# A two-layer transformer-like stack on one core: six phi(q) buffers, two norms moved to VectorE, the first load split, one output unit moved

## The chip, the cores and the metric

The kernel runs on one core of one Trainium2 chip. The metric is the device time in microseconds (us) of one execution, the median of several runs. The engines are named as the profile names them: PE is TensorE (matmuls), PEld its weight loads, DVE is VectorE, ACT is ScalarE, POOL is GpSimd, SP is SyncE, which here only issues DMAs. "SPq" and "ACTq" are the issuing queues.

## The reference

Four layers over x of 2048 rows and 1024 columns: linear attention A, gated bilinear unit B, and both once more with the same weights. Each is added to x after a layer norm.

```python
def _A_ref(x, wqkv, wo):                       # 32 heads of 32
    q, k, v = split_heads(x @ wqkv)
    phi = lambda t: jnp.where(t > 0, t + 1, jnp.exp(t)) + 1e-6
    pq, pk = phi(q), phi(k)
    kv = jnp.einsum("bhsd,bhse->bhde", pk, v)
    z = jnp.einsum("bhsd->bhd", pk)
    num = jnp.einsum("bhqd,bhde->bhqe", pq, kv)
    den = jnp.einsum("bhqd,bhd->bhq", pq, z)[..., None] + 1e-6
    return merge_heads(num / den) @ wo
def _B_ref(x, w_gate, w_up, w_down):           # 1024 -> 3584 -> 1024
    g, u = x @ w_gate, x @ w_up
    return (g * u) @ w_down
x = x + _A_ref(_layernorm(x), A_wqkv, A_wo)
x = x + _B_ref(_layernorm(x), B_w_gate, B_w_up, B_w_down)
x = x + _A_ref(_layernorm(x), A_wqkv, A_wo)
x = x + _B_ref(_layernorm(x), B_w_gate, B_w_up, B_w_down)
```

Head splitting and merging are written as names here.

## The kernel before

All buffers are placed by hand in a few large tiles (K0 to K7, W, MX, TX, ST, XT0, XT1), PSUM is used as eight banks Q0 to Q7, and the order of the instructions on each engine is the order in which the Python code emits them. x stays in SBUF as X, 16 row tiles of 128 x 1024, in four groups of four tiles. Each tile's normalised rows are transposed by a DMA (tx, L301, issued on SP), for the first few tiles on PE.

**A layer of A** (layer_A, layers 0 and 2) runs: the k units (32, a tile and a half of the columns each); then xk units, phi(k) transposed times the normalised x; then 32 q units, q[2t] and q[2t+1] for the two halves of tile t. A q unit is eight matmuls into one bank (proj_mm, L340), then phi: ACT takes the exponential (L328, or L323 and L324 in the "split" form), DVE finishes it (L329 and L330, or L325 and L326) into the tile's buffer from pqb. Each q unit then calls flush, which runs one half of the previous tile's division: den_sums (L420 to L423) after q[2t], den_divide (L428) and the transpose of the buffer after q[2t+1]. The buffers of pqb are taken in turn; so a tile's first phi write waits until the transpose of the tile that had the buffer before has read it.

With the q units of the last five tiles the kernel mixes the "kv copies" (kvo_unit: one matmul L447 into Q5 to Q7 in turn, and a scaled copy by ACT, L448) and the first output units. An output unit o[i] is eight matmuls (L459) and add_x on DVE (L451), which adds the bank into X. There are 32; the first six are ordered so that three with n = 0 come first. PE's banks come from mm_tile, a running count taken modulo rotation[0]: five while the kv copies use Q5 to Q7, eight otherwise.

Other work is hung on the output units. jobs[i] runs after o[i]: in layer 0, o[2] to o[8] each bring one scan (scan_step, L217: ACT squares a 512 KB chunk of weights and sums it; 42 chunks, the last ones w_down, each fetched by a DMA issued on ACT, L209, into a buffer that an earlier scan leaves), o[3] to o[6] the conversion of the first gate and up weights (L489) and their sums (L492), o[10] and o[15] the scale of w_down from the scans (scale_sum, L226 and L227; scale_pow, whose matmul is L232, then POOL's power L234). The list norm holds the layer norms of groups 0 and 1 for the next layer, one step after each of o[8] to o[17], the rest spread over o[18] to o[27]. For each tile a norm on ACT (ln_act) is three passes over the tile (L285 mean, L289 variance, L295 apply), between them small POOL steps (L286, L290 to L292), and then the transpose. The form used elsewhere, ln_stats and ln_apply, has DVE take statistics (L251, L255), POOL two steps (L257, L259), and DVE apply (L269).

**A layer of B** (layer_B, layers 1 and 3) computes its three matrix products by a scheme with seven half-size products instead of eight. At its start the products 1 and 2 (L527) use group 0's transposed x; the products 6 and 5 use sums of the two groups, t_fill (L492, into TX). After products 1, 6 and 7 ACT copies the banks (L545, L549) into SN, which lies in MX and W. MX is otherwise used in layer A for zb, its first quarter; its other three quarters are free there.

Of the kernel before, what the change touches and what calls it, by code (L numbers as in the profile page):

```python
# [37 lines left out]
def kernel(  # L38
# [11 lines left out]
    nc = tc.nc  # L50
    P = 128
    S, D = A_x.shape[1], A_x.shape[2]
# [8 lines left out]
    TPG = G // P  # L61
    NB = 512
# [12 lines left out]
    X = const.tile([P, NT, D], BF16, tag="X", name="X")  # L75
# [3 lines left out]
    MX = const.tile([P, 4 * D], BF16, tag="MX", name="MX")  # L79
    K = [const.tile([P, BLK], BF16, tag=f"K{i}", name=f"K{i}") for i in range(8)]  # L80
    W = const.tile([P, 8 * D], BF16, tag="W", name="W")
# [8 lines left out]
    def tail(i, j):  # L90
        return K[i][:, HEAD + j * D:HEAD + (j + 1) * D]
# [9 lines left out]
    pk = [tail(0, 2)] + [tail(i, j) for i in (1, 2, 3, 4, 5) for j in range(3)]  # L101
    sk = K[0][:, HEAD:HEAD + 2 * D].bitcast(F32)
    zb = MX[:, 0:D]
    pqb = [W[:, i * D:(i + 1) * D] for i in range(3)]
    pb = [W[:, 6 * D + i * NB:6 * D + (i + 1) * NB] for i in range(4)]
    eb = [W[:, 3 * D + i * NB:3 * D + (i + 1) * NB] for i in range(3)]
    kvt = W[:, 5 * D:6 * D].rearrange("p (c f) -> p c f", f=P)
# [4 lines left out]
    xn_c = {TPG + i: tail(i, 0) for i in range(4)}  # L112
    xn_b = [ST[:, t % TPG * D:(t % TPG + 1) * D] for t in range(NT)]
# [6 lines left out]
    count = {}  # L120
# [5 lines left out]
    x_view = A_x[0].rearrange("(t p) d -> p t d", p=P)  # L126
# [7 lines left out]
    def load(dst, src):  # L134
        nc.sync.dma_start(out=dst, in_=src)
# [9 lines left out]
    def load_x(t):  # L145
        load(X[:, t, :], x_view[:, t, :])

    load_x(0)
    load_x(1)
    for k in range(0, KD, 2):  # L150
        load(wk[0][:, k:k + 2, :], wqkv_v[:, k:k + 2, D:D + NB])
# [96 lines left out]
    def bn(t, c):  # L248
        if c == 0:
            stat[t] = [small.tile([P, 2, 6], F32, tag="st", name="st")]  # L250
        nc.vector.bn_stats(out=stat[t][0][:, c, :], in_=X[:, t, c * NB:(c + 1) * NB])  # L251

    def moments(t):
        mv = small.tile([P, 2], F32, tag="mv", bufs=2 * TPG, name="mv")
        nc.vector.bn_aggr(out=mv[:], in_=stat[t][0][:])  # L255
        ve = small.tile([P, 1], F32, tag="ve", name="ve")
        nc.gpsimd.tensor_scalar(out=ve[:], in0=mv[:, 1:2], scalar1=1e-5, scalar2=None, op0=ALU.add)  # L257
        rstd = small.tile([P, 1], F32, tag="rstd", bufs=2 * TPG, name="rstd")
        nc.gpsimd.tensor_tensor(out=rstd[:], in0=ve[:], in1=mhalf[:, 0:1], op=ALU.pow)  # L259
        stat[t] = (mv, rstd)  # L260

    def ln_stats(t):
        bn(t, 0)
        bn(t, 1)
        moments(t)

    def ln_apply(t, xn):
        mv, rstd = stat.pop(t)
        nc.vector.tensor_scalar(out=xn, in0=X[:, t, :], scalar1=mv[:, 0:1], scalar2=rstd[:],  # L269
                                op0=ALU.subtract, op1=ALU.mult)  # L270
# [9 lines left out]
    def ln_act(t, xn):  # L280

        sm, nm, ss, ve, rstd, off = (small.tile([P, 1], F32, tag=n_, name=n_) for n_ in ("sm", "nm", "ss", "va", "rs", "of"))

        def mean():
            nc.scalar.activation(out=xn, in_=X[:, t, :], func=ACT.Identity, accum_out=sm[:])  # L285
            nc.gpsimd.tensor_scalar(out=nm[:], in0=sm[:], scalar1=-1.0 / D, scalar2=None, op0=ALU.mult)  # L286

        def var():
            nc.scalar.activation(out=xn, in_=X[:, t, :], func=ACT.Square, bias=nm[:], accum_out=ss[:])  # L289
            nc.gpsimd.tensor_scalar(out=ve[:], in0=ss[:], scalar1=1.0 / D, scalar2=1e-5, op0=ALU.mult, op1=ALU.add)  # L290
            nc.gpsimd.tensor_tensor(out=rstd[:], in0=ve[:], in1=mhalf[:, 0:1], op=ALU.pow)
            nc.gpsimd.tensor_tensor(out=off[:], in0=nm[:], in1=rstd[:], op=ALU.mult)  # L292

        def apply():
            nc.scalar.activation(out=xn, in_=X[:, t, :], func=ACT.Identity, scale=rstd[:], bias=off[:])  # L295
        return mean, var, apply

    def tx(xn, t, slot):

        tl = t % TPG  # L300
        nc.sync.dma_start_transpose(out=xT[slot][:, :, tl * P:(tl + 1) * P], in_=xn)  # L301
# [106 lines left out]
    def flush():  # L408
        if later:
            later.pop(0)()  # L410
# [43 lines left out]
    def out_unit(t, n):  # L454
        def run():
            ps = mm_tile()
            tl = t % TPG
            for c in range(KD):
                nc.tensor.matmul(out=ps, lhsT=xT[t // TPG][:, c, tl * P:(tl + 1) * P].bitcast(F16), rhs=KVo[n][:, c, :],  # L459
                                 start=(c == 0), stop=(c == KD - 1))  # L460
            add_x(t, n, ps)
        return run
# [41 lines left out]
    def prep(n, eng=nc.vector):  # L504
        return [lambda: convert(n, 0), lambda: convert(n, 1), lambda: sums(n, 0, eng), lambda: sums(n, 1, eng)]
# [96 lines left out]
    def do(units):  # L602
        for u in units:
            u()
# [12 lines left out]
        tr = [lambda t=t: tx(dst[t], t, slot_) for t in ts]  # L617
        return st + [ap[0], ap[1], tr[0], ap[2], tr[1], ap[3], tr[2], tr[3]]

    def norm_act(g, slot_, dst):  # L620

        f = [ln_act(t, dst[t]) for t in range(g * TPG, (g + 1) * TPG)]
        tr = [lambda t=t: tx(dst[t], t, slot_) for t in range(g * TPG, (g + 1) * TPG)]
        out_ = []
        for i in range(TPG + 2):
            for j, k in ((i, 0), (i - 1, 1), (i - 2, 2)):
                if 0 <= j < TPG:
                    out_.append(f[j][k])
                    if k == 2:
                        out_.append(tr[j])  # L630
        return out_
# [3 lines left out]
    def layer_A(li):  # L635
# [103 lines left out]
        kvo = [lambda c=c: kvo_unit(c % KD, c // KD) for c in range(2 * KD)]  # L739
        o = [out_unit(t, n) for t in range(NT) for n in range(2)]  # L740
        o = [o[i] for i in (0, 2, 4, 1, 3, 5)] + o[6:]
        norm = norm_act(0, 0, xn_b) + norm_act(1, 1, xn_c)
        jobs = {3: prep(0)[0:1], 4: prep(0)[1:2], 5: prep(0)[2:3], 6: prep(0)[3:4]}
        if first_A:
            for i, f in ((10, lambda: scale_sum(2, 3)), (9, dp[0][0]), (15, lambda: scale_pow(2, 3)), (13, dp[1][0])):
# [4 lines left out]
        def out_next(n=1):  # L750
            for _ in range(n):
                i = count["o"] = count.get("o", -1) + 1
                o[i]()
                do(jobs.get(i, []))
                if 8 <= i < 18:
                    do(norm[i - 8:i - 7])
# [3 lines left out]
        for i in range(6):  # L760
            q[22 + i]()
            do(kvo[8 * i // 3:8 * (i + 1) // 3])
            if i > 2:
                out_next()
        rotation[0] = 8
        for i in range(4):
# [2 lines left out]
        flush()  # L769
        out_next()  # L770
        flush()
        out_next(6)
        down = list(dp[0][1:]) + list(dp[1][1:]) if first_A else []
        late = norm[10:]
        for i in range(10):
# [16 lines left out]
    def layer_B(li):  # L792
        last = li == 3
        R = [Q[2 * i:2 * i + 2] for i in range(4)]
        for ps in range(2):
# [165 lines left out]
            R = [R[2], R[1], R[3], R[0]]  # L961

    layer_A(0)
    layer_B(1)
    layer_A(2)
    layer_B(3)

# [29 lines left out]
```

## Time and profile before

| | us |
|---|---|
| median of 3 runs | 1499.27 (1498.31 to 1500.75) |
| the profiled execution, its own time | 1501.54 |
| its span, first to last instruction | 1499.8 |
| PE busy | 1485.4 |
| DVE busy | 1053.0 |
| ACT busy | 747.2 |

Where the stages of the profiled execution lie: layer 0 to 248.3 us, layer 1 to 759.6, layer 2 to 989.0, layer 3 to the end. The granted clock of PE is 0.999 in the mean. The page gives each engine's busy time and its share of the span; since PE's is 99%, what can be read from the waits is where the remaining time lies, and from the windows where the clock was not full.

### The profile page before, as it was taken

How to read it: one execution, taken by the hardware profiler on the slowest of the kernel's cores; microseconds unless marked ns; L12 is line 12 of the kernel's file. 1: busy time of each engine (PE TensorE's matmuls, PEld its weight loads, DVE VectorE, ACT ScalarE, POOL GpSimd, SP SyncE). 2: the span in 40 equal slices, each digit the busy share in tenths (PEclk: the TensorE clock that was granted, in tenths of full speed). 3: DMA queues.
4: the chain of work that ended last, by engine and by line, in shares of the span. 5: the costliest groups of instructions: out<-in, count | busy, mean ns of one | idle time of the engine just before them, and what ended most of it. 6: DMA issues, size and time to landing. Idle time of an engine off the chain costs nothing.

```text
span 1499.8 us, 18432 instructions
## 1 busy us (share of the span) xinstructions
PE 1485.4 (99%) x6997; PEld 676.1 (45%) x6997; DVE 1053.0 (70%) x1813; ACT 747.2 (50%) x934; POOL 67.3 (4%) x187
## 2 busy tenths in 40 slices
PE   9999999999999999999999999999999999999999
PEld 3444444444444444444444444444444444444444
DVE  7768767888866577767388567667776846777533
ACT  4988587777601366650022446846664015666300
POOL 3100002000000000001010000200000100000000
PEclk9999999999999999999999999999999999999999
DMA  7966947667647333336660115433333763333442
GB/s 216 248 190 179 233 93 197 200 200 212 195 163 216 84 85 85 85 127 175 183 168 1 20 33 124 69 94 85 91 95 110 211 190 97 85 84 85 147 167 86
DMA packets 276905, 202.80 MB, mean 135 GB/s; under 512 B 101968, under 2 KB 264016, under 8 KB 273232
## 3 DMA queue, kind: packets, MB, share of 16 engines
q1 hardware_dynamic: 261456, 182.74, 43.8%
q10 hardware_dynamic: 15360, 18.88, 4.2%
q8 instruction: 55, 0.90, 0.3%
q14 instruction: 34, 0.28, 0.1%
HBM read 160.43 MB, written 17.04 MB: 118 GB/s over the span
## 4 chain that ended last, share of the span: by engine, by line
PE 82%; ACT 2%; DVE 1%; issue 1%; DMA 1%; POOL 0%; SPq 0%; ACTq 0%; DVEq 0%
PE Q L527 45%; PE Q L828 23%; PE Q L340 7%; PE Q L459 4%; PE Q L355 4%; ACT K L217 0%; DMA K<-in_B_w_down_dram 0%; DVE X L451 0%; ACT K L289 0%; PE Q L439 0%; ACT K L285 0%; DMA XT<-K 0%; ACT K L448 0%; ACT W L324 0%; DVE den L421 0%
## 5 line engine op out<-in xcount | busy, mean ns | idle before, releaser
L527 PEld LDWEIGHTS <-K 128*128 128x128 f16 x3136 | 306.7, 98 | 373.6 <-issue 2.4
L527 PE MATMUL Q<-XT,K 128*128 128x512 bf16 (+1 forms) x1792 | 405.7, 379 | 0.0
L828 PE MATMUL Q<-K,K 128*128 128x512 f16 (+2 forms) x1582 | 340.4, 377 | 0.0
L527 PE MATMUL Q<-TX,K 128*128 128x512 f16 x1344 | 308.4, 379 | 2.8 <-ACT W L549 1.4
L489 ACT ACTIVATE K<-K,fac 128x2048 f16<-128x2048 bf16 x112 | 218.4, 2000 | 128.1 <-DMA K<-in_B_w_gate_dram 127.2
L828 PEld LDWEIGHTS <-K 128*128 128x128 f16 x1582 | 154.3, 98 | 184.5
L492 DVE TENSOR_TENSOR K<-K 128x1024 f16<-128x1024 f16 (+1 forms) x244 | 157.3, 666 | 34.2 <-ACT K L489 32.3
L492 DVE TENSOR_TENSOR W<-MX,Q 128x512 f16<-128x512 f32 x176 | 116.4, 684 | 30.0 <-ACT MX L549 18.6
L328 ACT ACTIVATE W<-Q 128x512 bf16<-128x512 f32 x90 | 52.8, 595 | 137.7 <-PE Q L340 127.9
L340 PE MATMUL Q<-K,K 128*128 128x512 bf16 x512 | 115.6, 380 | 3.6 <-DVE X L451 3.6
L549 ACT COPY MX<-Q 128x512 f32<-128x512 f32 x120 | 69.2, 584 | 96.0 <-PE Q L527 96.0
L340 PE MATMUL Q<-K,XT 128*128 128x512 bf16 x512 | 114.6, 379 | 1.4 <-DMA XT<-ST 0.7
L492 DVE TENSOR_TENSOR W<-W,Q 128x512 f16<-128x512 f32 x160 | 105.4, 684 | 13.3 <-ACT W L549 7.1
L549 ACT COPY W<-Q 128x512 f32<-128x512 f32 x104 | 60.3, 584 | 73.5 <-PE Q L527 73.4
L492 DVE TENSOR_TENSOR K<-K,K 128x512 f16<-128x512 f16 (+1 forms) x148 | 87.7, 597 | 4.2
L492 DVE TENSOR_TENSOR K<-W,Q 128x512 f16<-128x512 f16 x56 | 38.4, 686 | 71.9 <-PE Q L527 71.9
L340 PEld LDWEIGHTS <-K 128*128 128x128 bf16 x512 | 49.9, 98 | 64.1 <-issue 4.7
L835 DVE SCALAR_TENSOR_TENSOR W<-Q,kap,X 128x512 f32<-128x512 f32 x32 | 24.0, 750 | 77.6 <-PE Q L828 77.6
L340 PEld LDWEIGHTS <-XT 128*128 128x128 bf16 x512 | 49.5, 98 | 61.1 <-ACT XT L316 1.4
L531 DVE TENSOR_TENSOR K<-W 128x512 f16<-128x512 f16 x168 | 71.4, 425 | 5.8
L217 ACT ACTIVATE K<-K 128x2048 bf16<-128x2048 bf16 x37 | 70.6, 1908 | 3.4 <-DMA K<-in_B_w_down_dram 2.4
L545 ACT COPY MX<-Q 128x512 f32<-128x512 f32 x56 | 32.3, 588 | 63.4 <-PE Q L527 63.4
(111 smaller groups left out, 1226.3 us busy)
## 6 DMA issues: line engine op xcount, KB each, us to landing
K<-WD SPq DMA_DIRECT2D x28, 1792.0 KB, 7.4
K<-in_B_w_gate_dram SPq DMA_DIRECT2D x70, 512.0 KB, 4.2
K<-in_B_w_up_dram SPq DMA_DIRECT2D x56, 512.0 KB, 5.1
K<-in_A_wqkv_dram SPq DMA_DIRECT2D x10, 1024.0 KB, 7.8
K<-in_B_w_up_dram ACTq DMA_DIRECT2D x12, 512.0 KB, 4.0
K<-in_B_w_down_dram ACTq DMA_DIRECT2D x11, 512.0 KB, 4.6
K<-in_B_w_down_dram SPq DMA_DIRECT2D x10, 512.0 KB, 5.4
WD<-K SPq DMA_DIRECT2D x10, 512.0 KB, 3.0
```

What stands on the lines that cost most here:

```text
L217: nc.scalar.activation(out=scan_buf[i], in_=scan_buf[i], func=ACT.Square, accum_out=acc[:, m, c:c + 1])
L328: nc.scalar.activation(out=e, in_=ps, func=ACT.Exp)
L340: nc.tensor.matmul(out=ps, lhsT=xt[:, k, tl * P:(tl + 1) * P], rhs=w[:, k, :], start=(k == 0), stop=(k == KD - 1))
L355: nc.tensor.matmul(out=ps, lhsT=xn_a[t][:, j * P:(j + 1) * P], rhs=pk[t][:, n * NB:(n + 1) * NB], start=(t == 0), stop=(t == NT - 1))
L459: nc.tensor.matmul(out=ps, lhsT=xT[t // TPG][:, c, tl * P:(tl + 1) * P].bitcast(F16), rhs=KVo[n][:, c, :], start=(c == 0), stop=(c == KD - 1))
L489: nc.scalar.activation(out=b.bitcast(F16), in_=b, func=ACT.Copy, scale=fac[:, m:m + 1])
L492: eng.tensor_tensor(out=o, in0=a, in1=b, op=op)
L527: nc.tensor.matmul(out=pair[m], lhsT=stationary(n, p, m, k), rhs=moving[p][:, k, :], start=(p in (1, 2, 5) and k == 0), stop=(k == KH - 1) ...
L531: nc.vector.tensor_tensor(out=hA[i][:, u, :], in0=gu[:, 0, :], in1=gu[:, 1, :], op=ALU.mult)
L545: nc.scalar.copy(out=snaps[u, 1][:, m, :], in_=a[m])
L549: nc.scalar.copy(out=snaps[u, p][:, m, :], in_=a[m])
L828: nc.tensor.matmul(out=ps_[:, lo:hi], lhsT=act[:, u, j * P:(j + 1) * P], rhs=w[:, u, lo:hi], start=(p in (1, 2, 5) and u == 0), stop=(u == ...
```

## The change

Four edits.

1. pqb has six buffers instead of three: the three in W, and the three free quarters of MX.
2. The first tile of x is loaded as two halves of 512 columns, one issued on SP as before, the other on ACT.
3. norm_act gets a number m: the first m tiles of the group take the norm on ACT, the others ln_stats and ln_apply on DVE, in the same steps of the list. Group 0 keeps all four tiles on ACT, group 1 only two.
4. While the kv copies run, an output unit follows q[25] and q[27] but no longer q[26]. All later pairs of output units thus begin one unit earlier in number, and after the second flush seven units follow instead of six, so that 18 have run before the loop over o[18 + i].

```diff
-    pqb = [W[:, i * D:(i + 1) * D] for i in range(3)]
+    pqb = [W[:, i * D:(i + 1) * D] for i in range(3)] + [MX[:, i * D:(i + 1) * D] for i in range(1, 4)]
...
-    load_x(0)
+    nc.sync.dma_start(out=X[:, 0, 0:NB], in_=x_view[:, 0, 0:NB])
+    nc.scalar.dma_start(out=X[:, 0, NB:D], in_=x_view[:, 0, NB:D])
...
-    def norm_act(g, slot_, dst):
-
-        f = [ln_act(t, dst[t]) for t in range(g * TPG, (g + 1) * TPG)]
-        tr = [lambda t=t: tx(dst[t], t, slot_) for t in range(g * TPG, (g + 1) * TPG)]
+    def norm_act(g, slot_, dst, m):
+
+        ts = range(g * TPG, (g + 1) * TPG)
+        f = [ln_act(t, dst[t]) for t in ts[:m]]
+        f += [(lambda t=t: ln_stats(t), lambda: None, lambda t=t: ln_apply(t, dst[t])) for t in ts[m:]]
+        tr = [lambda t=t: tx(dst[t], t, slot_) for t in ts]
...
-        norm = norm_act(0, 0, xn_b) + norm_act(1, 1, xn_c)
+        norm = norm_act(0, 0, xn_b, TPG) + norm_act(1, 1, xn_c, 2)
...
             do(kvo[8 * i // 3:8 * (i + 1) // 3])
-            if i > 2:
+            if i == 3 or i > 4:
                 out_next()
         rotation[0] = 8
...
         flush()
         out_next()
         flush()
-        out_next(6)
+        out_next(17 - count["o"])
```

## The prediction, made before the change was run

> **What bounds the kernel now.** I read the page first, then the waits by engine, then the timeline around every place where TensorE waits. The page:
>
> ```profile
> PE 1485.4 (99%) x6997; PEld 676.1 (45%) x6997; DVE 1053.0 (70%) x1813; ACT 747.2 (50%) x934; POOL 67.3 (4%) x187
> ```
>
> The span is 1499.8 us, so TensorE idles for only 14.4 us. Nothing that shortens DVE or ACT work as such can pay; only an idle gap of TensorE, or matmuls run at a lower clock, can be won. The waits, by engine and line (us in total, times, longest):
>
> ```profile
> DVE W L330 <- DMA K<-W: 4.1, 2, 2.8
> ...
> PE Q L340 <- DVE X L451: 3.6, 1, 3.6
> PE Q L527 <- ACT W L549: 1.4, 2, 1.2
> PE Q L527 <- DVE TX L492: 1.3, 1, 1.3
> ...
> PE Q L459 <- DVE W L330: 0.8, 1, 0.8
> ```
>
> Both waits on DVE work of 3.6 and 0.8 us lie in the first attention layer, where the kv copies and the last q units run together. Timeline of DVE and of TensorE there (start, length, instruction, idle before it and who ended it):
>
> ```profile
> 171.83 0.69 DVE L330 SCALAR_TENSOR_TENSOR W<-Q,W 128x512 bf16<-128x512 f32 x1 [1.30 <-DMA K<-W]
> 179.97 0.69 DVE L330 SCALAR_TENSOR_TENSOR W<-Q,W 128x512 bf16<-128x512 f32 x1 [2.79 <-DMA K<-W]
> ...
> 184.04 1.89 PE L459 MATMUL Q<-K,XT 128*128 128x512 bf16 x8 [0.80 <-DVE W L330]
> 189.50 2.44 PE L340 MATMUL Q<-K,K 128*128 128x512 bf16 x8 [3.57 <-DVE X L451]
> 191.73 4.79 PE L459 MATMUL Q<-K,XT 128*128 128x512 bf16 x16
> ```
>
> L330 writes phi(q) of tile 11 (and 12) into the buffer that tile 8 (and 9) left, and waits for that tile's transpose to be read out. In that stretch the transposes land late: "DMA to landing" of L301 between 150 and 260 us is
>
> ```profile
> DMA to landing us min/median/max: 3.0/4.3/10.0
> ```
>
> DVE is otherwise back to back from 165 to 191, so the 1.30 + 2.79 = 4.09 us push everything behind. Then the clock, by windows (window, us, busy time of each engine, granted clock, DMA share, GB/s):
>
> ```profile
> 184.00:188.00 4.00, 1.89 (x8) 0.78 (x8) 3.87 (x6) 1.54 (x3) 0.00 (x0) 1.00 0.34 66
> 188.00:192.00 4.00, 2.50 (x9) 1.04 (x9) 3.73 (x8) 1.80 (x1) 0.00 (x0) 0.84 0.00 0
> 192.00:196.00 4.00, 4.00 (x15) 1.61 (x14) 2.89 (x6) 3.55 (x7) 0.00 (x0) 0.74 0.34 66
> ```
>
> After the 3.57 us gap the granted clock is 0.84 and 0.74. The step into layer 1:
>
> ```profile
> 248.31 3.62 PE L527 MATMUL Q<-XT,K 128*128 128x512 bf16 x16
> 253.19 2.98 PE L527 MATMUL Q<-TX,K 128*128 128x512 f16 x13 [1.26 <-DVE TX L492]
> ...
> 250.18 1.22 DVE L492 TENSOR_TENSOR TX<-XT,XT 128x2048 f16<-128x2048 bf16 x1 [2.71 <-DMA XT<-K]
> ```
>
> The norms of the second group end late on ACT, their transposes land at 249.9, and the first sum waits. In layer 2 (ACT, the kv copies L448):
>
> ```profile
> 926.81 1.84 ACT L448 ACTIVATE K<-Q,rz 128x512 bf16<-128x512 f32 x3
> 929.85 0.60 ACT L323 ACTIVATE W<-Q 128x512 bf16<-128x512 f32 x1 [1.19 <-PE Q L340]
> ```
>
> Here ACT waits for TensorE, and TensorE has no gap beyond 0.2 us.
>
> **What the Trainium skill says.** "TensorE: Matmul & The Clock Gate", section "What's actually happening": after an idle window of about 3.4 us the clock falls to half. The trace agrees: lower clock after 3.57 us, none after 1.26 us. "Perfetto Trace Analysis", section "Tensor Engine Instruction": ACT, DVE and GpSimd are strict first-in-first-out; the 4.09 us that pass through L330 to everything behind it agree. "DMA: Bandwidth & Descriptors", section "Issuing engines are not separate DMA queues": issuing from another engine saves only issue time.
>
> **The change, part by part.** Pitches, start to next start, from the timelines: L329 0.33, L330 0.61, the den sums L420 to L423 2.46, L428 1.13, L325 0.38, L326 0.34, add_x 0.60 us; a q or out unit 1.727, a kv matmul 0.216, L323 0.49, L324 0.57, a kv copy 0.61 us.
>
> *Six buffers.* Tiles 11 and 12 now overwrite what tiles 5 and 6 left, long transposed. Both DMA waits go, and DVE is 4.09 us earlier from q unit 24 on: L330 of q25 at 183.30 − 4.09 = 179.2, add_x of the first out unit at 180.95, q26's L326 at 181.92, its den sums done at 184.7. The ACT inputs were ready before (L323 at 178.47). The 0.80 us wait goes.
>
> *The out unit moved from q26 to behind q28.* TensorE in layer 0: q26 176.54, three kv to 178.9, q27 at once to 180.64, three kv. Their banks (three in turn) come free with ACT's copies at 179.53 to 181.37, so the third kv waits 0.35. Out unit 2 ends at 183.4; q28 follows. By the bank counts (q22 is the 81st tile; five in rotation, then eight) q28 now takes bank 0 (q26's, read by 179.6) and no longer the bank of the second out unit, on which it waited 3.57. That bank falls to the unit after next, o3: ready 186.83, add_x done at 187.3, 0.45 us. Before, nine units and eight kv matmuls, 15.54 + 1.73 = 17.27 us, took 172.66 to 196.36 = 23.70; now they take 17.27 + 0.80. Gain 5.6 us, about 2.1 of it the clock.
>
> *What is late next.* ACT's chain of squares over w_down (scans 35 to 41) moves one out unit later in order: scan 35 behind q28's L326, 188.0 instead of 190.2. In pitches (scan 2.0, convert 2.0, DMA issue 0.4) ACT then runs: scans 35 and 36, issue, convert to 194.4; q29's pair to 195.5; scan 37, issue of fetch 39 at 197.5, convert, scan 38, issue of fetch 40 at 201.9; q30's pair at 202.3; scan 39 at 203.5 when its fetch lands, issue of fetch 41 at 205.5; scan 40 206.0; q31's pair 207.95; scan 41 at 209.2 when its fetch lands, to 211.1 instead of 215.4. Fetch to landing in this stretch was 3.6, 3.7, 6.0 and 6.1 us, the long ones behind a transpose; I take 6.0 for fetch 39 and 3.7 for 40 and 41, bounds 3.6 and 10.1 (the longest of L209). The scale sum now stands behind the den sums of tile 15 (one more out unit precedes q31's followers): from q31's L323 to L326 1.19, then 0.34, L428 1.13, add_x twice 1.2, den sums 2.46, add_x 0.6, L226 and L227 0.4, together 7.3: partb at 215.3; TensorE reaches its matmul L232 at 214.9. Stall 0.35 (before 0.1); 2.3 if all three fetches take 6.0. All banks in between come free over 1 us early by the same table. So the last out unit ends at 215.3 + 16 × 1.727 = 242.9 instead of 248.31: 5.4 us.
>
> *Two norms on DVE.* ACT loses 2 × 3.6 us (1.04 + 1.14 + 1.23 and the accumulator reads); DVE gets 2 × (1.3 + 0.2 + 0.55) = 4.1 us, covered by the 1.04 us it idles before each out unit's add_x at 240 to 247. Without that cover out banks would come free later, eight deep. The wait added: POOL's ve of tile 6 stands behind DVE's aggregate (DVE: scale_pow's steps to 221.0, then add_x of units 16 to 22, 4.2, and the down weights' sums of two units, 4.4, to 229.6; stats 1.5: 231.1) and holds tile 5's three POOL steps, so tile 5's apply runs 232.9 to 234.2 on ACT. DVE applies tile 7 at about 237.3. SP then holds transposes 5, 6, 7, with the loads of unit 1 (1 MB) ahead; with the 4.75 us from L295's end to landing seen before (245.14 to 249.89) the last lands at 242. The two sums end at 245.0; the product wants them at 242.9 + 3.62 = 246.5. The 1.26 us gap goes, 1.5 us to spare.
>
> *Layer 2.* The same code, other banks. TensorE: q26 923.82, kv to 926.2, q27 to 927.92; the third kv waits for a copy that ends 928.65, out unit 2 ends 930.7. q28 is there the 207th tile, bank 6, which is the last kv's: ACT copies it only after q27's L323 and L324, at 928.65 + 1.06 + 1.84 = 931.55. q28 starts 931.6; with one out unit less before it, the order of before would have had 932.02 − 1.73 = 930.29. Loss 1.3 us, in full, since nothing later has slack. Bounds 0 and 1.5.
>
> *First x tile.* The half on SP lands at best 0.3 us before 3.37 (half the bytes). But the second transposes on TensorE (8.87) hang on tile 2, issued at 2.62 and landed at 7.65, whose bytes and place stay: nothing, bounds −0.3 and +0.3.
>
> Sum: −5.4 − 1.26 + 1.3 = −5.35 us on a profiled execution of 1501.54 us (span 1499.8), itself 2.3 above the median. On the median, 1499.27 − 5.3 = 1494.0.
>
> **The rivals.**
> A, forecast: 1494.0, own range 1492.3 to 1496.2 (the stall at L232 up to 2.3, the 0.5 us waits of layer 1 on L549 either way).
> B, a transfer takes the gap's place: tile 7's transpose takes 10.0 us as the worst did. It lands at 247.3, sums end at 250.2, the product loses 3.7 of the 6.7 us: −3.0 + 1.3 = 1497.6. For it: 1 MB of loads just ahead. Against it: the same loads stood there before, landing 3.3 us.
> C, ACT keeps ahead of the kv matmuls in both layers (copies on time): 1494.0 − 1.3 − 0.8 − 0.35 = 1491.6. Against it: 3.1 us of ACT per q against 2.4 of TensorE without an out unit.
> D, slower: the w_down fetches land as slowly as 10.1 us. Scan 41 then ends at 221.6, partb at 222, TensorE stalls 7.1 and loses 2 of clock; the norms follow 10.5 us later, the product starts at 255.2 against 253.19, plus layer 2: 1502.6. It decides from about 8.5 us on. Against it: the four fetches here took 3.6 to 6.1.
>
> **Numbers.** A 0.60, B 0.22, C 0.11, D 0.07. A measurement can tell about 0.2%, 3.0 us, from no change. Faster: nearly all of A, and C: 0.70; within: B and A's tail, 0.22; slower: D, 0.08. The range 1491.3 to 1497.6 leaves out D and the edges of B and C.
>
> **What would show it.** Right: no L330 wait on DMA; no gap over 1 us at 180 to 192, clock 1.00 there; L527 about 243; no wait of L527 on L492; q28 of layer 2 waiting 0.9 us on L448. Wrong: TensorE waiting over 2 us at L232, or the first sums still waiting on XT's transposes, or no wait in layer 2.

## The result, and the profile after

The kernel after took 1493.91 us (median of 6 runs, 1493.56 to 1494.89), the kernel before, on the same chip, 1499.89 us (6 runs, 1498.31 to 1500.97). The ratio is 0.9961 with a 95% interval of 0.9948 to 0.9974: faster by 0.26 to 0.52%. The forecast was 1494.0 us, and faster. The profiled execution took 1494.89 us with a span of 1493.1; that of before had 1501.54 and 1499.8.

In the kernel after, line numbers are one higher than in the kernel before from L149 on (L340 is L341, L527 is L528), and three higher from the body of norm_act on (L828 is L831). Output units are numbered from zero, o[0] to o[31]. First the busy times of its page:

```profile
PE 1477.1 (99%) x6895; PEld 675.9 (45%) x6997; DVE 1060.9 (71%) x1829; ACT 734.7 (49%) x914; POOL 66.4 (4%) x179
```

TensorE is still the bound, with 8.3 us less busy time (part of it records missing from the trace: 6895 matmuls against 6997) and 16.0 us idle. VectorE has 7.9 us more and ScalarE 12.5 us less, the norms that changed engines.

The place in layer 0 where TensorE used to wait, from TensorE's timeline of the kernel after (start, length, instruction, in brackets the idle time before it and who ended it):

```profile
178.56 1.89 PE L341 MATMUL Q<-K,K 128*128 128x512 bf16 x8
...
181.08 0.38 PE L448 MATMUL Q<-TX,W 128*128 128x512 bf16 x1 [0.19 <-ACT K L449]
...
183.02 1.89 PE L341 MATMUL Q<-K,K 128*128 128x512 bf16 x7
...
187.01 1.89 PE L460 MATMUL Q<-K,XT 128*128 128x512 bf16 x8 [0.37 <-DVE X L452]
...
214.63 0.16 PE L233 MATMUL Q<-partb,ones 128*128 128x1 bf16 x1
...
242.28 3.62 PE L528 MATMUL Q<-XT,K 128*128 128x512 bf16 x16
245.74 2.54 PE L528 MATMUL Q<-TX,K 128*128 128x512 f16 x11
```

The gaps of 0.80 and 3.57 us have become 0.19 (the third kv matmul, on the copy L449) and 0.37 (o[3], on the bank that add_x reads). L233, the scale's matmul, shows no wait. Layer 1 starts at 242.28 instead of 248.31, and its second product, which needs the sums of the norms, follows 3.46 us later without the gap of 1.26. The clock, in the windows of the kernel after (window, us, busy time by engine, granted clock, DMA share, GB/s):

```profile
184.00:188.00 4.00, 3.57 (x17) 1.56 (x16) 3.77 (x9) 1.47 (x3) 0.00 (x0) 1.00 0.10 20
188.00:192.00 4.00, 4.00 (x21) 1.80 (x19) 3.17 (x6) 3.60 (x4) 0.00 (x0) 1.00 0.24 46
192.00:196.00 4.00, 3.95 (x19) 1.83 (x19) 1.14 (x3) 3.95 (x4) 0.00 (x0) 1.00 0.38 131
```

The 0.84 and 0.74 of before are 1.00.

The two transposes of tiles 8 and 9 are as late as before: from issue to landing they take 9.7 and 9.3 us, in the kernel before 10.0 and 9.5. What went is only the wait of VectorE for their buffers. The loads of the output weights and of layer 1's first weights are in flight in the same stretch; whether they are what makes the transposes late, and whether loads at another time would do as well as more buffers, was not tried.

In layer 2, TensorE's timeline of the kernel before:

```profile
932.02 1.89 PE L340 MATMUL Q<-K,K 128*128 128x512 bf16 x8
```

and of the kernel after:

```profile
920.44 0.38 PE L448 MATMUL Q<-TX,W 128*128 128x512 bf16 x1 [0.19 <-ACT K L449]
920.65 1.89 PE L460 MATMUL Q<-K,XT 128*128 128x512 bf16 x8
923.24 1.89 PE L341 MATMUL Q<-K,K 128*128 128x512 bf16 x7 [0.70 <-ACT K L449]
```

q28 (932.02 before, 923.24 after) now waits for the last kv copy, which in the kernel before it didn't: a loss, as forecast.

To compare profiles I cut each at the same four TensorE starts: q25 of layer 0, the first product that needs the norms' sums (L527 from TX), layer 2's first k unit, and the first product of layer 3. All times in us:

| | before | after | difference |
|---|---|---|---|
| start to q25 | 172.66 | 172.30 | −0.36 |
| q25 to the product with the sums | 80.53 | 73.44 | −7.09 |
| on to layer 2 (all of layer 1) | 506.24 | 505.40 | −0.84 |
| layer 2 | 229.57 | 230.80 | +1.23 |
| layer 3 to the end | 510.75 | 511.17 | +0.42 |
| span | 1499.75 | 1493.11 | −6.64 |

Called below "the stretch" is the second row; its first part, q25 to layer 1's first product, went from 75.65 to 69.98. Each of these times is read from one profiled execution. Kernels that should agree in a row do: the stretch is 73.41 to 73.44 us in the kernel after, e3, e4, e5, e8 and e9, and layer 2 is 229.57 to 229.59 in every kernel with the old order there.

### The profile page after: what moved, and what is told of

Same layout as the page of the kernel before. It is cut to its first block, busy times and chain, and to the rows that moved or that the text cites. A ratio compares the mean times of both kernels' runs of the same rounds, so it can differ in the third digit from the quotient of the medians.

```text
span 1493.1 us, 18319 instructions
## 1 busy us (share of the span) xinstructions
PE 1477.1 (99%) x6895; PEld 675.9 (45%) x6997; DVE 1060.9 (71%) x1829; ACT 734.7 (49%) x914; POOL 66.4 (4%) x179
## 4 chain that ended last, share of the span: by engine, by line
PE 86%; ACT 1%; issue 0%; DVE 0%; ACTq 0%
PE Q L528 45%; PE Q L831 23%; PE Q L341 7%; PE Q L460 7%; PE Q L356 4%; ACT K L449 0%; PE Q L440 0%; ACT W L324 0%; PE Q L448 0%; PE Q L382 0%; ACT W L325 0%; ACT W L550 0%; DVE X L838 0%; PE Q L392 0%; ACTq L324 0%
## 5 line engine op out<-in xcount | busy, mean ns | idle before, releaser
L528 PEld LDWEIGHTS <-K 128*128 128x128 f16 x3136 | 306.9, 98 | 371.2 <-issue 1.3
L528 PE MATMUL Q<-XT,K 128*128 128x512 bf16 (+1 forms) x1734 | 398.7, 379 | 3.1
L831 PE MATMUL Q<-K,K 128*128 128x512 f16 (+2 forms) x1582 | 340.4, 377 | 0.0
L528 PE MATMUL Q<-TX,K 128*128 128x512 f16 x1344 | 308.3, 379 | 1.1 <-ACT W L550 1.1
L831 PEld LDWEIGHTS <-K 128*128 128x128 f16 x1582 | 154.3, 98 | 184.5
L550 ACT COPY MX<-Q 128x512 f32<-128x512 f32 x120 | 69.2, 585 | 96.4 <-PE Q L528 96.4
L341 PE MATMUL Q<-K,XT 128*128 128x512 bf16 x500 | 113.9, 379 | 2.3 <-DMA XT<-ST 0.9
L341 PE MATMUL Q<-K,K 128*128 128x512 bf16 x497 | 113.8, 379 | 1.4 <-ACT K L449 0.7
L341 PEld LDWEIGHTS <-K 128*128 128x128 bf16 x512 | 50.0, 98 | 61.0 <-issue 1.5
L341 PEld LDWEIGHTS <-XT 128*128 128x128 bf16 x512 | 49.4, 98 | 61.4 <-ACT XT L317 1.4
L252 DVE BATCH_NORM_STATS2 st<-X 128x6 f32<-128x512 bf16 x104 | 66.0, 675 | 3.1 <-DMA X<-in_A_x_dram 3.1
```

What stands on the lines that cost most here:

```text
L341: nc.tensor.matmul(out=ps, lhsT=xt[:, k, tl * P:(tl + 1) * P], rhs=w[:, k, :], start=(k == 0), stop=(k == KD - 1))
L528: nc.tensor.matmul(out=pair[m], lhsT=stationary(n, p, m, k), rhs=moving[p][:, k, :], start=(p in (1, 2, 5) and k == 0), stop=(k == KH - 1) ...
L550: nc.scalar.copy(out=snaps[u, p][:, m, :], in_=a[m])
L831: nc.tensor.matmul(out=ps_[:, lo:hi], lhsT=act[:, u, j * P:(j + 1) * P], rhs=w[:, u, lo:hi], start=(p in (1, 2, 5) and u == 0), stop=(u == ...
```

## The experiments

Each was timed beside the kernel before on the same chip; ratios are to that. The diffs show what was changed against the kernel named. Two questions: which of the four edits carries the 7.09 us, and what took the gap in front of the products with the sums away. My theory after the result was the forecast's own, by its steps: the buffers and the place of the unit give the stretch, and the split of the norms closes the gap.

### One edit alone, or one edit undone

**e1: the kernel before with six buffers, nothing else.**

```diff
-    pqb = [W[:, i * D:(i + 1) * D] for i in range(3)]
+    pqb = [W[:, i * D:(i + 1) * D] for i in range(3)] + [MX[:, i * D:(i + 1) * D] for i in range(1, 4)]
```

> The kernel before with six phi(q) buffers and nothing else. Theory: both DMA waits of L330 go, DVE is 4.1 us earlier, the wait of q unit 28 falls from 3.57 us to about 0.5, the clock stays at 1.00, and the last out unit of layer 0 ends near 242.6 instead of 248.3. But all eight norms stay on ACT, which ends them about 4.0 us earlier, not 5.7, so the first product of layer 1 that needs the sums waits about 2.9 us on L492 instead of 1.26. Layer 2 loses nothing. Sum about 1499.9 - 4.1 = 1495.8 us, a bit less if the small waits of layer 1 shrink too. Rival: the buffers are the whole gain, the other edits add nothing: 1493.9 or, without the loss in layer 2, 1492.7, and no wait over 1.3 us on L492.

Measured: 1495.21 us (1493.98 to 1497.38), ratio 0.9968, 0.9955 to 0.9981. TensorE's timeline:

```profile
185.58 1.89 PE L340 MATMUL Q<-K,K 128*128 128x512 bf16 x8 [0.58 <-DVE X L451]
...
248.48 3.63 PE L527 MATMUL Q<-TX,K 128*128 128x512 f16 x16 [1.76 <-DVE TX L492]
```

The wait of 3.57 us shrank to 0.58 at the same unit, q28. The stretch took 75.73 us, 4.80 less than before; the wait on the norms' sums (L492) is still there, 1.76 us instead of 1.26, though not the 2.9 us that I expected. Layer 2 took 229.58, as before.

**e2: the kernel after, with the old order of the output units among the kv copies.**

```diff
-            if i == 3 or i > 4:
+            if i > 2:
```

> The changed kernel with the out unit back behind q unit 26. Theory: the move costs in layer 2 and brings nothing in layer 0. Layer 2: the waits of TensorE on the kv copies (0.70 us before q28 and 0.2 us before the last kv matmul) go, 1.2 us. Layer 0: q28 waits about 0.75 us on L452 where the changed kernel waits 0.37 + 0.19; no clock dip. Sum 1493.9 - 1.0 = 1492.9 us. Rival: the moved unit is what frees q28's bank in layer 0; without it q28 waits over 3 us, the clock falls, and the time is 1496 us or more.

Measured: 1496.18 us (10 runs, 1494.49 to 1498.83), ratio 0.9973, 0.9962 to 0.9984. The expectation missed. The median is the rival's, but not for its reason: q28 waits 0.58 us, not 3. Layer 2 took its 229.58 us again, so the loss there is the moved unit's. But the stretch took 75.58, and the product waited 1.57 us on the sums, although two of the norms ran on VectorE. TensorE's timeline:

```profile
248.51 3.63 PE L528 MATMUL Q<-TX,K 128*128 128x512 f16 x16 [1.57 <-DVE TX L493]
```

The split of the norms doesn't close the gap. Why not is on ScalarE's timeline of e2, tile 5's apply:

```profile
235.71 1.24 ACT L296 ACTIVATE K<-X,of,rs 128x1024 bf16<-128x1024 bf16 x1 [2.90 <-POOL of L293]
```

ScalarE, though it has half the work, stands for 2.90 us: GpSimd does tile 6's steps first, and those wait for VectorE's statistics. Tile 5's apply, and with it the transposes behind it, is no earlier than with all norms on ScalarE (235.71, in e1 235.12).

**e3: the kernel after with four buffers instead of six** (`range(1, 2)` in place of `range(1, 4)`).

> The changed kernel with four phi(q) buffers instead of six. Theory: only the transposes of tiles 8 and 9 are late, by one tile's time; with four buffers tile 11 overwrites tile 7's and tile 12 tile 8's, both read out by then. No wait of L331 on a DMA, 1493.9 us within 0.5. Rival: the late transposes hold DVE for longer than one tile, so each buffer up to six counts: waits of L331 on a DMA of 1 us or more, 1495 us or more.

Measured: 1494.32 us, ratio 0.9964, 0.9951 to 0.9976; stretch 73.42, layer 2 230.80. One more buffer than three is enough.

**e4: the kernel after with all norms on ScalarE.**

```diff
-        norm = norm_act(0, 0, xn_b, TPG) + norm_act(1, 1, xn_c, 2)
+        norm = norm_act(0, 0, xn_b, TPG) + norm_act(1, 1, xn_c, TPG)
```

> The changed kernel with all four norms of the second group on ACT. Theory: ACT is then busy without a break from the last scan at 210.7 for 29.7 us, the last transpose lands at about 245.1, the sums end at 248.4 where the product wants them at 245.8: a wait of 2.6 us on L493 at the start of layer 1, 1493.9 + 2.6 = 1496.5 us. Rival: the norms are hidden, ACT has room since the scans end earlier: wait under 0.5 us, 1494.0 us.

Measured: 1494.14 us (1493.07 to 1495.36), ratio 0.9960, 0.9947 to 0.9974. The wait that I expected isn't there; the rival was right. The stretch took 73.42 us against 73.44 of the kernel after. The first sum started at 242.16 with four norms on ScalarE, at 241.87 with two. What holds the last transposes is SyncE's queue. Its issues in e4 (start, length of the issue; tiles 5, 6 and 7):

```profile
234.52 2.54 SPq L302 DMA_TRANSPOSE XT<-K  x1
237.17 1.29 SPq L302 DMA_TRANSPOSE XT<-K  x1
238.57 1.25 SPq L302 DMA_TRANSPOSE XT<-K  x1
```

and in the kernel after, behind the second half of the 1 MB that load_unit(1, 1) fetches:

```profile
232.89 0.75 SPq L135 DMA_DIRECT2D K<-in_B_w_up_dram  x1
233.75 2.88 SPq L302 DMA_TRANSPOSE XT<-K  x1
236.75 1.52 SPq L302 DMA_TRANSPOSE XT<-K  x1
238.37 1.25 SPq L302 DMA_TRANSPOSE XT<-K  x1
```

Tile 5's issue takes 2.54 and 2.88 us behind that load, where an issue with nothing close ahead takes 1.23. The last one starts 66.07 us after q25 in the kernel after and 66.51 in e4. So, counted from q25, the two norms on VectorE were worth 0.4 us at this point, and nothing at TensorE.

**e6: the kernel after with three buffers** (the diff of e1 undone).

> The changed kernel with three phi(q) buffers: the other three edits without the first. Theory: the two waits of L331 on a DMA are back (about 4 us), the add_x that frees the bank of the out unit after q28 comes 4.1 us later, TensorE waits there about 4.3 us instead of 0.37 and the clock falls for some 2 us. From q unit 25 to the first product that needs the sums about 79.4 us instead of 73.4, layer 2 at 230.8: about 1499.9 us, no gain on the kernel before. Rival: the moved unit frees q28's bank by itself, so most of the gain stays: 1496 us or less.

Measured: 1500.43 us (12 runs), ratio 0.9998, 0.9990 to 1.0006: without the buffers, the other three edits are worth nothing together in the time. The wait of VectorE on the transposes is back, from the waits of e6:

```profile
DVE W L331 <- DMA K<-W: 3.8, 2, 2.8
```

and in TensorE's timeline the late add_x now stops o[3] instead of q28:

```profile
190.67 3.03 PE L460 MATMUL Q<-K,XT 128*128 128x512 bf16 x8 [4.10 <-DVE X L452]
193.50 2.48 PE L341 MATMUL Q<-K,K 128*128 128x512 bf16 x8
```

The eight matmuls behind it take 3.03 us instead of 1.89: the clock fell. The stretch is 78.85 us, 1.68 less than before, since the wait on the sums is gone here too; layer 2 gives 1.23 of it back.

**e5: the kernel after, the unit moved in layer 0 only.**

```diff
-            if i == 3 or i > 4:
+            if i == 3 or i > 4 or (i == 4 and not first_A):
```

> The changed kernel with the out unit moved in layer 0 only; layer 2 keeps the order of before. Theory: layer 0 stays as in the changed kernel (from q unit 25 to the first product that needs the sums 73.4 us), layer 2 (first k unit to the first product of layer 3) falls from 230.80 to 229.58 us, as in the kernels with the old order. Sum 1493.9 - 1.2 = 1492.7 us. Rival: the order of layer 2 is not the cause, the six buffers or the norms on DVE are: layer 2 stays at 230.8 us, 1493.9 us.

Measured: 1492.56 us (1492.20 to 1493.99), ratio 0.9945, 0.9933 to 0.9957. Stretch 73.42, layer 2 229.59: all of the gain and none of the loss.

**e8: the kernel after, with one PSUM bank skipped in the count of layer 2.**

```diff
+        if not first_A:
+            mm_tile()
```

> The changed kernel with one tile of the bank count skipped in layer 2 before q unit 22, so that q28 gets bank 7 instead of 6. Nothing else differs. Theory: q28 waits for the last kv copy only because it has that copy's bank; with bank 7 it needs a copy that ends 1.2 us earlier. Its wait of 0.70 us on L449 goes, the 0.2 us of the last kv matmul stays; layer 2 falls from 230.80 to about 230.1 us, 1493.2 us. Rival: the missing out unit as such leaves ACT behind, whatever the bank: layer 2 stays at 230.8 us.

Measured: 1495.28 us, ratio 0.9958, 0.9944 to 0.9972. Half of the expectation held: q28 starts at 922.66 without a wait, so the collision of banks is what it waited on. But layer 2 still took 230.88 us, because the shifted count collides at the layer's other end, on TensorE's timeline:

```profile
922.66 1.89 PE L341 MATMUL Q<-K,K 128*128 128x512 bf16 x7
...
982.32 1.89 PE L528 MATMUL Q<-XT,K 128*128 128x512 bf16 x8 [0.79 <-DVE X L452]
```

The first product of layer 3 takes a bank that the last add_x still reads.

**e9: the kernel before with two edits, six buffers and e5's place of the unit;** all norms on ScalarE, x loaded whole.

> The kernel before with two edits alone: six buffers, and the output unit moved among the kv copies in layer 0 only; all norms stay on ScalarE and the first x tile is loaded whole. Theory (the shared norms and the halves add nothing): from the first product of layer 0's q25 to the first that needs the norms' sums 73.4 us, as in e5, layer 2 in 229.6 us, no wait over 1 us of the products on the norms, and a median of 1492.2 to 1492.9 us. Rival (the norms' split is needed beside the order): a wait over 1 us on ScalarE's norms, 74.8 us or more in that stretch, 1493.9 us or more.

Measured: 1493.95 us (1492.11 to 1494.63), ratio 0.9951, 0.9939 to 0.9963. Stretch 73.41 and layer 2 229.58, no wait on the sums: this part of the theory stands, and the median alone sits on the rival's side, within its interval of e5's. TensorE's timeline at layer 1's start:

```profile
242.87 3.62 PE L527 MATMUL Q<-XT,K 128*128 128x512 bf16 x16
246.32 3.62 PE L527 MATMUL Q<-TX,K 128*128 128x512 f16 x16
```

The profile puts the difference elsewhere. Layer 1 took 506.19 us against e5's 505.35, with one wait of 1.39 us on ScalarE's bank copy at 291 us (in e5 1.01) that other executions of the same layer code show as 1.1, 0.6 or not at all. I see nothing in these edits that reaches there, and its cause stays open. So the split of the norms adds nothing in the stretch that it was written for, and neither do the halves.

### Why the moved unit closes the gap

e1 and e9 differ in one output unit's place, and that removed 2.32 us of the stretch, 1.76 of them the wait on the norms. Four runs asked how.

**e7: e1 with load_unit(1, 1) issued three units earlier** (`i == 2` for `i == 5`).

> The kernel before with six buffers, and the weights of unit 1 loaded after out unit 20 instead of 23, ahead of the last transposes by three units; all norms on ACT, old order. Theory: the last transposes are late because tile 5's stands on SP's queue directly behind this 1 MB load and takes 2.5 to 3.3 us to issue instead of 1.25; without it the last one is issued about 2 us earlier, when its tile is ready, and the wait of 1.76 us on L492 goes: from q unit 25 to that product 74.0 us instead of 75.7, 1493.5 us. Rival: ACT's norms bind, not the queue: the wait stays above 1.2 us, 1495.2 us.

Measured: 1494.69 us, ratio 0.9958, 0.9946 to 0.9971. The wait fell to 1.07 us only, the stretch to 74.81, between the theory and its rival. The stores of the scaled w_down (WD) now stood behind the load, the second pair 3.04 us in the issuing, and the four transposes together took 6.4 from 236.17 on.

**e10: the load issued ahead of all norm transposes.**

```diff
+        load_unit(1, 1)
         out_next(6)
...
-            if i == 5:
-                load_unit(1, 1)
```

> e1 (six buffers, old order, all norms on ScalarE) with unit 1's weight load issued before the sixth output unit, ahead of all the norm transposes. Theory A (the load in front of tile 5's transpose in SyncE's queue holds the sums): tile 5's transpose takes about 1.3 us to issue instead of 3.2, the wait of the products on the norms falls from 1.76 to under 0.3 us, and the stretch from q25 to the first product that needs the sums is about 73.9 us; median about 1493.6 us. Theory B (the norms on ScalarE bind, behind GpSimd's stores): the wait stays near 1 us as in e7, the stretch at 74.8 us, the median at 1494.7 us.

Measured: 1496.23 us (1493.80 to 1496.93), ratio 0.9960, 0.9947 to 0.9974. Theory A falls: the wait is 1.91 us, the stretch 75.68. Tile 5's transpose did issue faster, in 1.85 instead of 3.17 us, but the queue was as late: its four transposes begin at 236.03, behind the WD stores, and run back to back to 243.16, the last one starting at 241.89 (e1: 241.98). Theory B's numbers (a wait near 1 us, 74.8 us) were missed too, and ScalarE wasn't the end of it: its last apply had ended at 239.7. Now the transposes of tiles 0 and 1 stand behind the moved load and take 1.96 and 3.19 us to issue (1.23 and 2.16 in e1), and from 220.62 on the queue's issues follow one another without a pause. In e1 the queue does pause before the stores: the transpose ahead of them ends at 226.55, the first store is issued at 227.63, for it needs w_down scaled, and the scale comes from GpSimd. ScalarE's timeline of e1 (the last scan, the first norm step, q31's phi, then the place where ScalarE stands):

```profile
208.22 1.91 ACT L217 ACTIVATE K<-K 128x2048 bf16<-128x2048 bf16 x1 [0.63 <-DMA K<-in_B_w_down_dram]
...
210.13 1.04 ACT L285 ACTIVATE ST<-X 128x1024 bf16<-128x1024 bf16 x1
...
211.17 0.57 ACT L323 ACTIVATE W<-Q 128x512 bf16<-128x512 f32 x1
...
222.83 1.15 ACT L289 ACTIVATE ST<-X,nm 128x1024 bf16<-128x1024 bf16 x1 [1.74 <-POOL nm L286]
```

and GpSimd's timeline of e1, the power for the scale:

```profile
222.05 0.55 POOL L234 TENSOR_TENSOR fac<-part,mhalf 128x1 f32<-128x1 f32 x1 [4.19 <-DVE part L233]
```

q31's phi stands behind the last scan. The scale's sum is cast on VectorE at 215.22, then come the den sums of tile 15 (2.5 us), the division and five add_x, and only then L233, which GpSimd waits 4.19 us for. In that time GpSimd holds the next norm's mean, and ScalarE stands for 1.74 us. In the kernel after the unit that is taken out makes q31 one unit earlier in the count: its phi comes before the last scan, and tile 15's den sums are done before the scale's sum.

**e11: e1 with one flush moved,** so that tile 15's den sums come before the scale's sum while q31 stays where it was.

```diff
         for i in range(4):
             q[28 + i]()
-            out_next(2)
+            out_next(2 if i < 3 else 1)
         flush()
-        out_next()
+        out_next(2)
         flush()
```

> e1 (six buffers, old order among the kv copies, all norms on ScalarE) with one flush moved: after q31 only one output unit runs, then the flush with the den sums of tile 15, then two. The scale sum thus stands behind those den sums on VectorE, as in the kernel after; nothing among the kv copies changes. Theory (the den sums, 2.46 us on VectorE between the scale sum and the step that GpSimd's fac waits for, hold fac, and with it ScalarE's norms and the stores and transposes in SyncE's queue): fac ends about 2.5 us earlier than in e1, ScalarE's wait of 1.74 us on GpSimd's nm shrinks to under 0.6, the products' wait of 1.76 us on the norms falls to under 0.5, q25 to the first product that needs the sums takes 73.9 to 74.4 us, the median is 1493.6 us; the wait of q28, 0.58 us, stays. Rival (the gap goes for a reason that lies among the kv copies): the wait stays above 1.2 us and the stretch at 75 us or more.

Measured: 1495.21 us (1494.37 to 1496.33), ratio 0.9964, 0.9952 to 0.9976. A miss, and its reason is instructive: the den sums can't start before q31's phi, which is late, so they pushed the scale's sum back instead. On TensorE:

```profile
217.22 0.18 PE L232 MATMUL Q<-partb,ones 128*128 128x1 bf16 x1 [2.58 <-ACT ST L295]
```

The row names ScalarE, whose apply had little to do with it; VectorE's timeline has the scale's cast, partb L227, from 217.00 to 217.16. The stretch became 77.72 us, 1.99 more than in e1, and the wait on the sums went to none only since TensorE itself was late. The median doesn't show these 2 us: it equals e1's, whose own runs spread over 3.4 us. In this comparison the stages of the profile say more than the medians.

**e12: e1 with the unit taken away between q30 and q31,** in both layers. Among the kv copies nothing changes.

```diff
         for i in range(4):
             q[28 + i]()
-            out_next(2)
+            out_next(1 if i == 2 else 2)
...
-        out_next(6)
+        out_next(7)
```

> e1 (six buffers, old order among the kv copies, all norms on ScalarE) with the output unit taken away between q30 and q31 instead of between q26 and q27, in both attention layers: everything among the kv copies stays as in e1, while q31 stands before output unit 8 (with the last scan and the first norm step), as in the kernel after. Theory (what removes the wait on the norms is q31's phi, ahead of the last scan and the first norm step on ScalarE, and with it the den sums of tile 15 ahead of the scale sum): GpSimd's fac ends about 2.4 us earlier in the layer than in e1, no wait over 0.4 us of the products on the norms, q28 still waits about 0.6 us, q25 to the first product that needs the sums 73.4 to 74.0 us, layer 2 in 229.6 us since nothing changes before q28 there, a median of 1492.5 to 1493.4 us. Rival (the gap goes for a reason among the kv copies): the wait on the norms stays above 1.2 us, the stretch at 75 us or more, 1495 us.

Measured: 1492.89 us (1491.86 to 1494.53), ratio 0.9947, 0.9933 to 0.9960. Everything as the theory had it. ScalarE's timeline of e12:

```profile
208.17 0.58 ACT L323 ACTIVATE W<-Q 128x512 bf16<-128x512 f32 x1
...
209.22 1.91 ACT L217 ACTIVATE K<-K 128x2048 bf16<-128x2048 bf16 x1
```

VectorE's timeline, the cast of the scale's sum and the step that GpSimd waits for, in e1:

```profile
215.22 0.16 DVE L227 CAST partb<-part 128x1 bf16<-128x1 f32 x1
...
221.82 0.15 DVE L233 TENSOR_SCALAR part<-Q 128x1 f32<-128x1 f32 x1
```

and in e12, where the den sums of tile 15 no longer stand between the two:

```profile
215.23 0.16 DVE L227 CAST partb<-part 128x1 bf16<-128x1 f32 x1
...
219.42 0.15 DVE L233 TENSOR_SCALAR part<-Q 128x1 f32<-128x1 f32 x1
```

GpSimd's:

```profile
219.65 0.55 POOL L234 TENSOR_TENSOR fac<-part,mhalf 128x1 f32<-128x1 f32 x1 [1.70 <-DVE part L233]
```

and TensorE's:

```profile
185.56 1.89 PE L340 MATMUL Q<-K,K 128*128 128x512 bf16 x8 [0.57 <-DVE X L451]
...
243.08 3.62 PE L527 MATMUL Q<-XT,K 128*128 128x512 bf16 x16
246.54 3.62 PE L527 MATMUL Q<-TX,K 128*128 128x512 f16 x16
```

q31's phi stands before the last scan, the power 2.40 us earlier than in e1 (222.05 to 219.65; q25 starts at 172.75 and 172.73), and ScalarE's 1.74 us on GpSimd's mean are gone. The wait on the sums is gone while q28's 0.57 us is as in e1. Stretch 73.81 us, 1.92 less than e1 and 0.4 more than the kernel after, and layer 2 229.58. This shows that the gap closes through q31's place and not through anything among the kv copies. That it is the den sums on VectorE, and not the order on ScalarE alone, is read from the timelines (the cast is at the same time, 215.22 and 215.23, and the power 2.40 us earlier); no run separates the two, since in e11, which was to do it, the scale's sum moved back with them.

e5 and e12 are the quickest kernels here. Both are ahead of the kernel after in the median, by 1.35 and 1.02 us, but their intervals overlap with its own; what is beyond doubt in every profile is the 1.2 us in layer 2.

## Why the prediction was right, and where it wasn't

The time was right, 1494.0 against 1493.91, but that close in part by luck: the forecast subtracted 5.3 from a median of 1499.27 of three runs, and the kernel before then came to 1499.89, a difference of 5.98. The profile's difference, −6.64 us, is 1.3 more than the sum of −5.35: 0.3 at the buffers and the unit, 0.2 at the gap, 0.1 in layer 2, and 0.8 in layer 1, which the sum didn't have; the start (−0.36) and the end (+0.42) cancel. By the steps:

- *Six buffers and the moved unit, −5.4 to the last output unit.* Right: 75.65 to 69.98 us, −5.67. Both VectorE waits on the transposes went, the clock stayed at 1.00, and e1 (70.35 with the buffers alone) and e6 (75.39 without them) show that the buffers carry it. The part called the clock's, 2.1 us, was 1.7: in the forecast's own lines 2.44 and 4.79 us instead of 1.89 and 3.62. The rest is that the trace counts a wait from the modelled end of the matmul before, 0.16 us after the next could have started (1.89 long, pitch 1.727). The small stalls were 0.19 for the third kv matmul (forecast 0.35), 0.37 at o[3] (0.45), none at the scale's matmul (0.35). The scans came as worked out: the last one at 208.81 on ScalarE, ending 210.7 for the forecast 211.1.
- *"Two norms on DVE … The 1.26 us gap goes".* The gap went (1.42 us from start to start: the second product follows 3.46 us after the first instead of 4.88), but the step is wrong; here the forecast was right by luck. With the split and the old order (e2) the gap is 1.57 us; with the new order and no split (e4, e9) there is none. The forecast's own sentence on GpSimd, that tile 6's step holds tile 5's three, was right (forecast apply 232.9, in the trace 232.29, after 1.68 us of standing). In the new order tile 5's apply still starts 1.2 us earlier with the split than without it (59.99 us after q25, in e4 61.21), but SyncE's queue leaves 0.4 us of that, and TensorE needs none of it. The effect that did it, as far as e12 and the timelines show, stood in the paragraph on what is late next: "The scale sum now stands behind the den sums of tile 15". I used it to place partb and stopped; that it also shortens the way from partb to GpSimd's power by the same 2.46 us, and with it ScalarE's norms and the stores in SyncE's queue, was not followed on. In e12 it is worth 2.40 us at the power and 1.92 at TensorE.
- *Layer 2, +1.3.* Right: +1.23, undone by e5. The bank named was the right one, as q28 lost its wait in e8. From o[1] to q28 it is 2.59 us start to start (920.65 to 923.24) where the pitch is 1.727: 0.86 us, for the forecast 0.9.
- *First x tile, nothing.* Consistent, with no run of its own. VectorE's first statistics start at 3.40 to 3.90 us in the seven profiles with halves and at 3.32 to 3.51 in the seven with the whole tile: the halves landed no earlier. That agrees with the sentence of the Trainium skill that the forecast used ("DMA: Bandwidth & Descriptors", "Issuing engines are not separate DMA queues"). The 0.36 us less up to q25 are within what the profiles show with the whole tile alone (q25 at 172.30 to 172.94).
- *Not in the sum.* Layer 1 was 0.84 us shorter and the last layer 0.42 longer. The first lies mostly at the waits on L549, which vary between executions: 1.15 and 0.27 us before, 1.06 after, none over 0.2 us in five of the fourteen profiles. The second appears in all six profiles with two norms on VectorE (511.15 to 513.33 us, the highest e2's) and in none of the eight others (510.74 to 510.82). It isn't in the norms' work: TensorE's starts in layer 3 agree to within 0.1 us up to its end (the kernel after and e4, e5 and e9, e2 and e1 compared), and the difference stands behind the landing of the last store, in the closing steps of the kernel (1.35 to 1.37 us in the six, 0.94 to 1.01 in the others). In e2 that store itself also landed 2.2 us later. Why the closing is longer stays open.

Of the rivals, B (a late transpose) and D (late w_down fetches) didn't occur, and neither did C: with the copies on time, the third kv matmul and layer 2's q28 wouldn't have waited.

## What to carry to other kernels

When several engines run in order and share small steps, count what stands between a producer and its consumer on the engine that carries both: here 2.46 us of den sums that moved from behind a sum to before it were worth more than giving half of a group's norms to another engine. A gap that closes in the result isn't proof of the edit that was meant to close it; undo that edit alone, and do it alone. A change of order that pays in one layer may meet another bank in the next, since the bank count runs on: look at every place where the code is used.

## What the runs showed of the hardware

- The clock fell after a shorter wait than I had thought. The forecast had 3.57 us with a dip and 1.26 without; the Trainium skill's page "TensorE: Matmul & The Clock Gate", "What's actually happening", speaks of an idle window of about 3.4 us. In e11 a wait of 2.58 us is followed by these windows (columns as above):

```profile
212.00:216.00 4.00, 2.64 (x13) 0.97 (x10) 3.90 (x6) 4.00 (x9) 2.08 (x5) 1.00 0.34 66
216.00:220.00 4.00, 2.78 (x9) 1.04 (x10) 3.97 (x9) 4.00 (x7) 0.95 (x3) 0.69 0.38 131
220.00:224.00 4.00, 3.95 (x17) 1.77 (x17) 3.23 (x11) 2.27 (x4) 2.11 (x7) 0.88 0.79 198
```

  The clock is 0.69 and 0.88; in windows of 0.5 us it is 0.50 to 0.55 from 217.5 to 221.0 and 1.00 on both sides. From q25 to layer 1's first product e11 took 3.92 us more than e1 (74.27 against 70.35), 2.23 of them the longer wait at L232 (2.58 against 0.35); the 1.7 left are half of those 3.5 us, about what the clock cost. Waits of 1.57, 1.76 and 1.91 us (e2, e1, e10) left the clock at 1.00. But the length of one wait doesn't decide it: at the start of e3 the clock fell around two shorter ones, as TensorE's timeline and a window show:

```profile
7.97 0.60 PE L341 MATMUL Q<-K,XT 128*128 128x512 bf16 x2 [0.68 <-ACT XT L317]
9.60 1.03 PE L314 MATMUL Q<-ident,TX 128*128 128x128 bf16 x8 [1.03 <-DVE TX L270]
...
8.00:12.00 4.00, 2.97 (x14) 1.50 (x15) 2.50 (x5) 1.41 (x2) 0.79 (x2) 0.67 1.08 365
```

  In e1, waits of 0.73, 0.68 and 0.41 us at the same place left it at 1.00. So these runs give no limit for one wait; short waits close together can cost the clock too, as in e3.
- A DMA transpose that SyncE issues right behind the two 512 KB halves of a load held the queue for 2.5 to 3.4 us (tile 5's, in the twelve profiles in which it stands there), one with nothing close ahead for 1.23. Right behind two 512 KB stores it was 2.3 to 3.1 us (tile 3's, in all fourteen), so moving the load away only moved the slow issue.
